# Loading w_up in two parts and regrouping the rows of w_down in a fused attention and feed-forward decode step

## The chip, the cores and the metric

One core of one Trainium2 chip runs the whole kernel in one launch. The metric is the device time of that core in microseconds, as a median over several executions. The six executions of the kernel before lie between 202.97 and 203.59 us, 0.3% or 0.6 us apart. The span that a profile shows is some 1.4 us shorter than the device time of the same execution (203.26 and 201.86 us before).

## The reference

A single token (640 features) goes through layernorm, attention over a cache of 32 heads with 4096 positions each, a residual, a second layernorm, and a gated feed-forward block with a residual. Weights and caches are bf16. Cut to what matters:

```
h  = x + attention(layernorm(x), k_cache, v_cache, wq, wo)
ln = layernorm(h)
g  = ln @ w_gate                 # 640 x 1728
u  = ln @ w_up                   # 640 x 1728
h2 = h + (gelu(g) * u) @ w_down  # 1728 x 640
```

With one token there is hardly any arithmetic per byte. The caches are 67 MB, all inputs together 84 MB, and each byte is used once.

## The kernel before

All large loads are issued by one engine (sync) on one queue (q1, 84.23 MB in the page), in the order wq, K and V caches by groups of four heads, wo, then the feed-forward weights. The feed-forward loads and the matmuls that use them are these; `P.dma(engine, out, in, *deps)` issues a transfer when its dependencies are done, and `T(fn, *deps)` runs matmuls when theirs are.

```python
d_w1 = P.dma("sync", wd_sb[:, 12, :], B_w_down[64:192, :], mults[NG - 1, 1])
for o in (0, 1, 2, 3, 32, 33, 34, 35):           # the first 64 rows of w_down, 8 loads of 10 KB
    ...
d_wg = P.dma("sync", wg_sb, B_w_gate[:, :].rearrange("(p c) n -> p c n", c=5), pvs[NG - 2])
d_wu = P.dma("sync", wu_sb, B_w_up[:, :].rearrange("(p c) n -> p c n", c=5))
d_wd = [P.dma("sync", wd_d[:, a, lo:hi, :], wd_v[:, a, lo:hi, :])
         for a, lo, hi in ((0, 0, 4), (1, 0, 4), (2, 0, 3), (2, 3, 4))]
... # cut: wo projection, second layernorm
def glu(ps, w, *ws):                             # 75 matmuls of one column each
    def fn(e):
        for c in range(5):
            for m in range(15):
                if m < 12:
                    ws = w[:, c, 192 + 512 * (m // 4) + m % 4:192 + 512 * (m // 4) + 512:4]
                elif m == 12:
                    ws = w[:, c, 64:192]
                else:
                    ws = w[:, c, 16 * m - 208:16 * m - 80]
                i = e.matmul(ps[:, m:m + 1], ws, hlnT[:, c:c + 1], ...)
        return i
    return T(fn, *ws)
ga = glu(ps_g, wg_sb, hl, d_wg)
up = glu(ps_u, wu_sb, d_wu)
... # cut: gelu on VectorE and ScalarE; hm = gelu(g) * u, needs ga and up
T(down([12]), g9, d_w1)                          # 4 matmuls per row block m, one per quarter of the output
T(down([13, 14]), d_wp)
T(down(range(4)), d_wd[0])
T(down(range(4, 8)), d_wd[1])
T(down(range(8, 11)), d_wd[2])
dn = {q: T(down([11], [q]), d_wd[3]) for q in (0, 2, 1, 3)}
... # cut: four copies of [1, 160] out of PSUM, two per engine; one store of the output row
```

A row of w_down is multiplied by one element of hm. Which partition a row of w_down lies in decides which column of w_gate and w_up must produce that element there, so regrouping the rows of w_down also changes the stride of the weights in `glu`.

The softmax here doesn't subtract the row's maximum and nothing guards it: scores larger than these inputs give would overflow.

Of the kernel before, what the change touches and what calls it, by code (L numbers as in the profile page):

```python
# [20 lines left out]
NG = 8  # L21
# [159 lines left out]
def bass_sequential_preLN__gqa_block_cached__glu_gated_geglu__decode_kernel(nc, A_x, A_k_cache, A_v_cache, A_wq, A_wo, B_x, B_w_gate, B_w_up, B_w_down, out):  # L181
# [49 lines left out]
    ps_g, ps_u, ps_p = bank[0], bank[1], bank[2]  # L231
# [10 lines left out]
    P = Prog(nc)  # L242
    V = lambda fn, *d: P.op("vector", fn, *d)
    A = lambda fn, *d: P.op("scalar", fn, *d)
    T = lambda fn, *d: P.op("tensor", fn, *d)
# [10 lines left out]
    mults, pvs = {}, {}  # L256
# [56 lines left out]
    def layernorm(src, ev, out_fn, between=lambda: None):  # L313
        s2 = V(lambda e: e.tensor_mul(src[:, 5:10], src[:, 0:5], src[:, 0:5]), ev)
        m = T(lambda e: e.matmul(ps_s[:, 16:26], mean_f[:, :], src[:, 0:10], start=True, stop=True), s2, c_mean)
        l1 = V(lambda e: e.reduce_sum(ln[:, 0:2], ps_s[:, 16:26].rearrange("p (a c) -> p a c", a=2), axis=AX.X), m)
        l2 = V(lambda e: e.scalar_tensor_tensor(out=ln[:, 2:3], in0=ln[:, 0:1], scalar=ln[:, 0:1],
                                                in1=ln[:, 1:2], op0=ALU.mult, op1=ALU.subtract), l1)
        l3 = A(lambda e: e.activation(ln[:, 3:4], ln[:, 2:3], ACTF.Ln, bias=eps_t[:, 0:1], scale=-1.0), l2, c_eps)
        l4 = A(lambda e: e.activation(ln[:, 4:5], ln[:, 3:4], ACTF.Exp, bias=zero_t[:, 0:1], scale=-0.5), l3)  # L320
        between()
        return V(out_fn, l4)
# [91 lines left out]
    for G in range(1, NG):  # L414
# [3 lines left out]
        for kind, g in order[3 + 2 * G:5 + 2 * G]:  # L418
# [8 lines left out]
                         start=True, stop=True), rt, c_ones)  # L427
# [7 lines left out]
                              start=True, stop=True), as_, c_of)  # L435
# [5 lines left out]
    wg_sb = v_slot[:, 0:5 * DF].rearrange("p (c n) -> p c n", c=5)  # L441
    wu_sb = v_slot[:, 5 * DF:10 * DF].rearrange("p (c n) -> p c n", c=5)
    wd_sb = k_slot[1][:, 0:15 * D].rearrange("p (m n) -> p m n", m=15)
    wd_v = B_w_down[192:1728, :].rearrange("(a p r) n -> p a r n", a=3, r=4)
    wd_d = wd_sb[:, 0:12, :].rearrange("p (a r) n -> p a r n", a=3)
    d_w1 = P.dma("sync", wd_sb[:, 12, :], B_w_down[64:192, :], mults[NG - 1, 1])
    for o in (0, 1, 2, 3, 32, 33, 34, 35):
        lo = o - o % 32
        d_wp = P.dma("sync", wd_lo[o:o + 13:4, :, :],
                     B_w_down[lo:lo + 32, :].rearrange("(r i q) n -> q i r n", q=4, r=2)[o - lo, :, :, :], c_wd, chan="wp")  # L450
    d_wg = P.dma("sync", wg_sb, B_w_gate[:, :].rearrange("(p c) n -> p c n", c=5), pvs[NG - 2])
    d_wu = P.dma("sync", wu_sb, B_w_up[:, :].rearrange("(p c) n -> p c n", c=5))
    d_wd = [P.dma("sync", wd_d[:, a, lo:hi, :], wd_v[:, a, lo:hi, :])
             for a, lo, hi in ((0, 0, 4), (1, 0, 4), (2, 0, 3), (2, 3, 4))]


    T(lambda e: e.matmul(ps_p[:, 0:5], id_f[:, :], xx[:, 0:5], start=True, stop=False, skip_group_check=True), xc, c_idf)
# [16 lines left out]
    def residual():  # L474
# [3 lines left out]
    hl = layernorm(hT, h, lambda e: e.tensor_scalar(  # L478
        hlnT[:, :], hT[:, 0:5], ln[:, 0:1], ln[:, 4:5], ALU.subtract, ALU.mult), residual)


    def glu(ps, w, *ws):
        def fn(e):
            for c in range(5):
                for m in range(15):
                    if m < 12:
                        ws = w[:, c, 192 + 512 * (m // 4) + m % 4:192 + 512 * (m // 4) + 512:4]
                    elif m == 12:
                        ws = w[:, c, 64:192]
                    else:  # L490
                        ws = w[:, c, 16 * m - 208:16 * m - 80]
                    i = e.matmul(ps[:, m:m + 1], ws, hlnT[:, c:c + 1],  # L492
                                 start=(c == 0 and m == 0), stop=(c == 4), skip_group_check=True)
            return i
        return T(fn, *ws)
    ga = glu(ps_g, wg_sb, hl, d_wg)

    up = glu(ps_u, wu_sb, d_wu)
    g1 = V(lambda e: e.tensor_tensor(out=g_t[:, :], in0=ps_g[:, 0:15], in1=own_g[:, :], op=ALU.mult), ga, c_gm)
    g2 = V(lambda e: e.tensor_mul(t1[:, :], g_t[:, :], g_t[:, :]), g1)  # L500
    g3 = V(lambda e: e.scalar_tensor_tensor(out=t2[:, :], in0=t1[:, :], scalar=1.0 / GELU_C1, in1=g_t[:, :],
# [5 lines left out]
    g9 = V(lambda e: e.tensor_mul(hm[:, :], gu[:, :], ps_u[:, 0:15]), g6, up)  # L507

    def down(ms, qs=range(4)):
        def fn(e):  # L510
            for m in ms:
                for q in qs:
                    rows, wd = (128, wd_sb[:, m]) if m < 13 else (48, wd_lo[:, m - 13])
                    i = e.matmul(ps_d[32 * q:32 * q + 1, 0:160], hm[0:rows, m:m + 1],  # L514
                                 wd[0:rows, 160 * q:160 * q + 160], start=False, stop=(m == 11))
            return i
        return fn
    T(down([12]), g9, d_w1)
    T(down([13, 14]), d_wp)
    T(down(range(4)), d_wd[0])  # L520
    T(down(range(4, 8)), d_wd[1])
    T(down(range(8, 11)), d_wd[2])
    dn = {q: T(down([11], [q]), d_wd[3]) for q in (0, 2, 1, 3)}
    os = [V(lambda e, q=q: e.tensor_copy(out_row[0:1, 160 * q:160 * q + 160], ps_d[32 * q:32 * q + 1, 0:160]), dn[q])  # L524
          for q in range(2)]
    os += [A(lambda e, q=q: e.copy(out_row[0:1, 160 * q:160 * q + 160], ps_d[32 * q:32 * q + 1, 0:160]), dn[q])
# [33 lines left out]
```

## Time and profile before

| | before |
|---|---|
| device time, median of 6 | 203.00 us (202.97 to 203.59) |
| span of the profiled execution (203.26 us) | 201.9 us |
| loaded from HBM | 84.23 MB, 417 GB/s over the span |
| busy: TensorE, VectorE | 60%, 50% |
| transfer engines | 97.6% |

In the views, PE is TensorE (matmuls), PEld its weight loads, DVE VectorE, ACT ScalarE, and SP the sync engine, which issues the large transfers. A transfer counts as landed here when the last of its completion counts in the trace has come; those of w_up came between 192.52 and 194.62 us in the trace before. Slack is the time between the landing of some data and the moment they are needed.

The page's chain of work that ended last, by line, names two loads and then compute. "L492" is `glu`, "L514" the down projection:

```profile
DMA v_slot<-in_A_v_cache_dram 55%; DMA v_slot<-in_B_w_up_dram 13%; PE psum L363 8%; DVE prod L375 7%; PE psum L167 6%; SPq L59 3%; DVE sc L381 2%; PE psum L492 1%; PE psum L514 1%; PE psum L352 1%; DVE out_row L524 0%; DVE hm L507 0%; DVEq L114 0%
```

The last load on it is w_up; the w_down loads issued behind w_up are not on it. The chain shows one path, the one that came last at each step, and hides how close the second was. The remaining lines, the utilisation and the timeline of the tail, stand in the prediction.

### The profile page before, as it was taken

How to read it: one execution, taken by the hardware profiler on the slowest of the kernel's cores; microseconds unless marked ns; L12 is line 12 of the kernel's file. 1: busy time of each engine (PE TensorE's matmuls, PEld its weight loads, DVE VectorE, ACT ScalarE, POOL GpSimd, SP SyncE). 2: the span in 40 equal slices, each digit the busy share in tenths (PEclk: the TensorE clock that was granted, in tenths of full speed). 3: DMA queues.
4: the chain of work that ended last, by engine and by line, in shares of the span. 5: the costliest groups of instructions: out<-in, count | busy, mean ns of one | idle time of the engine just before them, and what ended most of it. 6: DMA issues, size and time to landing. Idle time of an engine off the chain costs nothing.

```text
span 201.9 us, 2002 instructions
## 1 busy us (share of the span) xinstructions
PE 121.4 (60%) x1008; PEld 34.7 (17%) x756; DVE 100.9 (50%) x51; ACT 12.6 (6%) x33; POOL 30.6 (15%) x36
## 2 busy tenths in 40 slices
PE   0108009849408980994379166934990786779665
PEld 0101000001200120112011101020120012279563
DVE  0110197885598039906960993089519914120321
ACT  2010100001000100010000000100100010100101
POOL 6400000000010007101700450026006300100000
PEclk9999999999955698599579755995797599555555
DMA  9999999999999999999999999999999999999991
GB/s 341 422 425 435 429 422 429 416 474 425 429 422 422 422 448 448 435 416 429 422 422 474 422 429 422 429 416 474 429 429 416 429 422 444 402 419 444 428 387 61
DMA packets 3848, 84.30 MB, mean 418 GB/s; under 512 B 450, under 2 KB 772, under 8 KB 1156
## 3 DMA queue, kind: packets, MB, share of 16 engines
q1 hardware_dynamic: 3842, 84.23, 97.6%
q8 instruction: 4, 0.07, 0.1%
q10 hardware_dynamic: 2, 0.00, 0.0%
HBM read 84.23 MB, written 0.00 MB: 417 GB/s over the span
## 4 chain that ended last, share of the span: by engine, by line
DMA 68%; PE 18%; DVE 10%; SPq 3%; issue 1%; DVEq 0%
DMA v_slot<-in_A_v_cache_dram 55%; DMA v_slot<-in_B_w_up_dram 13%; PE psum L363 8%; DVE prod L375 7%; PE psum L167 6%; SPq L59 3%; DVE sc L381 2%; PE psum L492 1%; PE psum L514 1%; PE psum L352 1%; DVE out_row L524 0%; DVE hm L507 0%; DVEq L114 0%
## 5 line engine op out<-in xcount | busy, mean ns | idle before, releaser
L375 DVE TENSOR_TENSOR prod<-k_slot,qb 128x8192 bf16<-128x8192 bf16 x16 | 75.2, 4734 | 7.0 <-DMA k_slot<-in_A_k_cache_dram 5.2
L167 PE MATMUL psum<-prod,id_b 128*128 128x512 bf16 x233 | 65.4, 437 | 0.0
L381 DVE TENSOR_REDUCE sc<-psum 128x128 f32<-128x2048 f32 x8 | 18.3, 2291 | 49.1 <-PE psum L167 49.1
L352 PE MATMUL psum<-prod,id_b 128*128 128x512 bf16 x23 | 10.7, 467 | 50.5 <-DVE prod L375 47.1
L385 POOL TENSOR_TENSOR p_bd<-pt,own 128x512 bf16<-128x512 bf16 x6 | 24.4, 4071 | 89.5 <-ACT pt L382 89.5
L363 PE MATMUL psum<-v_slot,p_bd 128*16 128x512 bf16 x224 | 18.2, 484 | 5.1 <-DMA v_slot<-in_A_v_cache_dram 5.0
L352 PEld LDWEIGHTS psum<-prod,id_b 128*128 128x128 bf16 x23 | 2.3, 100 | 72.4 <-DVE prod L375 50.4
L369 PEld LDWEIGHTS psum<-hs,po_sb 128*128 128x128 f32 x64 | 9.1, 208 | 23.9 <-issue 23.4
L363 PEld LDWEIGHTS psum<-v_slot,p_bd 128*16 128x16 bf16 x224 | 5.8, 105 | 36.0 <-DMA v_slot<-in_A_v_cache_dram 27.9
L369 PE MATMUL psum<-hs,po_sb 128*128 128x4 f32 x64 | 8.5, 256 | 0.1
L392 ACT COPY po_sb<-psum 128x512 f32<-128x512 f32 x7 | 4.1, 586 | 71.8 <-PE psum L363 71.8
L382 ACT ACTIVATE pt<-sc,zero_t 128x128 bf16<-128x128 f32 x8 | 3.2, 401 | 71.2 <-DVE sc L381 71.2
L335 PE MATMUL psum<-arena,xlnB 128*32 128x512 bf16 x20 | 3.3, 627 | 6.2 <-DMA arena<-in_A_wq_dram 6.2
L462 PE MATMUL psum<-aP,arena 128*128 128x1 bf16 x160 | 6.7, 178 | 0.1
L462 PEld LDWEIGHTS psum<-aP,arena 128*128 128x128 bf16 x160 | 6.6, 131 | 0.2 <-DMA arena<-in_A_wo_dram 0.2
L492 PE MATMUL psum<-hlnT,v_slot 128*128 128x1 bf16 x150 | 5.1, 171 | 1.8 <-DMA v_slot<-in_B_w_up_dram 1.8
L389 POOL MEMSET spare<- 1x1 f32 x1 | 0.1, 90 | 36.6 <-DVE p_bd L385 36.6
L492 PEld LDWEIGHTS psum<-hlnT,v_slot 128*128 128x128 bf16 x150 | 5.0, 116 | 2.4 <-DMA v_slot<-in_B_w_up_dram 1.9
L308 PE MATMUL psum<-one_bf,x_row 1*128 1x1 bf16 x5 | 0.4, 177 | 8.3 <-DMA x_row<-in_A_x_dram 8.3
L363 PE MATMUL psum<-k_slot,p_bd 128*16 128x512 bf16 x32 | 3.6, 629 | 2.9 <-DVE p_bd L385 2.9
L340 DVE CAST qb<-psum 128x512 bf16<-128x512 f32 x1 | 0.7, 692 | 9.1 <-PE psum L167 9.1
L311 DVE COPY xx<-psum 128x5 f32<-128x5 f32 x1 | 0.2, 165 | 8.7 <-PE psum L308 8.7
(72 smaller groups left out, 35.1 us busy)
## 6 DMA issues: line engine op xcount, KB each, us to landing
k_slot<-in_A_k_cache_dram SPq DMA_DIRECT2D x8, 4096.0 KB, 25.5
v_slot<-in_A_v_cache_dram SPq DMA_DIRECT2D x7, 4096.0 KB, 16.7
arena<-in_A_wq_dram SPq DMA_DIRECT2D x1, 5120.0 KB, 15.8
arena<-in_A_wo_dram SPq DMA_DIRECT2D x2, 2560.0 KB, 34.5
k_slot<-in_A_v_cache_dram SPq DMA_DIRECT2D x1, 4096.0 KB, 26.1
v_slot<-in_B_w_gate_dram SPq DMA_DIRECT2D x1, 2160.0 KB, 21.3
v_slot<-in_B_w_up_dram SPq DMA_DIRECT2D x1, 2160.0 KB, 25.9
k_slot<-in_B_w_down_dram SPq DMA_DIRECT2D x2, 640.0 KB, 27.6
```

The costliest lines, as they stand in the source:

```text
L59: ev = self.op(eng, lambda e: e.dma_start(out, in_), *deps, dma=True, chan=chan)
L167: built = e.matmul(out, lhsT, rhs, start=start, stop=stop)
L335: mm = held if hf else lambda e, *a, **k: e.matmul(*a, **k)
L352: mm = held if n or not first else lambda e, *a, **k: e.matmul(*a, **k)
L363: i = e.matmul(ps_o[a:a + 16, :], p_bd[:, 4 * b:4 * b + 4, :].rearrange("p g j -> p (g j)"), vt[:, 4 * b:4 * b + 4, :], start=(b < 4), sto ...
L369: i = e.matmul(ps_a[:, bass.ds(at, 4)], po_sb[:, 128 * r:128 * r + 128], hs[:, r, :], start=(r == 0), stop=(r == 3))
L375: mults[G, i] = VM(lambda e: e.tensor_tensor(out=prod[:, i, :, :], in0=kt[:, 64 * i:64 * i + 64, :], in1=qb[:, G, :].unsqueeze(1).to_broad ...
L381: reds[G] = VR(lambda e: e.reduce_sum(sc[:, :], ps_f.rearrange("p (g d) -> p g d", d=16), axis=AX.X), folds[G, 1])
L385: blocks[G] = on(lambda e: e.tensor_tensor(out=p_bd[:, :, :], in0=pt[:, :].unsqueeze(2).to_broadcast([128, 128, 4]), in1=own[:, :].unsquee ...
L392: evs[G] = AS(lambda e: e.copy(po_sb[:, :], ps_o), pvs[G])
L462: r = e.matmul(ps_p[:, c:c + 1], wo_sb[:, i, c::5], aP[:, i:i + 1], start=False, stop=(i == 31), skip_group_check=True)
L492: i = e.matmul(ps[:, m:m + 1], ws, hlnT[:, c:c + 1], start=(c == 0 and m == 0), stop=(c == 4), skip_group_check=True)
```

## The change

Its intent is to shorten what can only start when w_up has landed: with w_up in two loads, three fifths of the up projection can run before the rest is in. And the rows of w_down, behind the first 64, are regrouped in blocks of 4, 4 and 5 rows per partition, so that the small load of rows 64 to 191 goes away. The diff, cut to its core:

```diff
-    d_w1 = P.dma("sync", wd_sb[:, 12, :], B_w_down[64:192, :], mults[NG - 1, 1])
+    blocks_d = ((64, 0, 4), (576, 4, 4), (1088, 8, 5))
+    at_row = {m0 + r: (lo + r, k) for lo, m0, k in blocks_d for r in range(k)}
+    def down_load(j, lo, hi): ...    # rows lo:hi of each partition of block j, after mults[NG - 1, 1]
...
-    d_wu = P.dma("sync", wu_sb, B_w_up[:, :].rearrange("(p c) n -> p c n", c=5))
-    d_wd = [P.dma("sync", wd_d[:, a, lo:hi, :], wd_v[:, a, lo:hi, :])
-             for a, lo, hi in ((0, 0, 4), (1, 0, 4), (2, 0, 3), (2, 3, 4))]
+    wu_v = B_w_up[:, :].rearrange("(p c) n -> p c n", c=5)
+    d_wu = [P.dma("sync", wu_sb[:, lo:hi, :], wu_v[:, lo:hi, :]) for lo, hi in ((0, 3), (3, 5))]
+    d_wd = [down_load(0, 0, 4), down_load(1, 0, 4), down_load(2, 0, 4), down_load(2, 4, 5)]
...
-                    if m < 12:
-                        ws = w[:, c, 192 + 512 * (m // 4) + m % 4:192 + 512 * (m // 4) + 512:4]
-                    elif m == 12:
-                        ws = w[:, c, 64:192]
+                    if m < 13:
+                        lo, k = at_row[m]
+                        ws = w[:, c, lo:lo + 127 * k + 1:k]
...
-    ga = glu(ps_g, wg_sb, hl, d_wg)
-    up = glu(ps_u, wu_sb, d_wu)
+    ga = glu(ps_g, wg_sb, range(5), hl, d_wg)
+    glu(ps_u, wu_sb, range(3), d_wu[0])
+    up = glu(ps_u, wu_sb, range(3, 5), d_wu[1])
...
-    T(down([12]), g9, d_w1)
-    T(down([13, 14]), d_wp)
+    T(down([13, 14]), g9, d_wp)
     T(down(range(4)), d_wd[0])
     T(down(range(4, 8)), d_wd[1])
-    T(down(range(8, 11)), d_wd[2])
-    dn = {q: T(down([11], [q]), d_wd[3]) for q in (0, 2, 1, 3)}
+    T(down(range(8, 12)), d_wd[2])
+    dn = {q: T(down([12], [q]), d_wd[3]) for q in (0, 2, 1, 3)}
```

More of the change, by code (lines that the diff above doesn't have):

```diff
@@ L443, in bass_sequential_preLN__gqa_block_cached__glu_gated_geglu__decode_kernel, with down_load @@
     wd_sb = k_slot[1][:, 0:15 * D].rearrange("p (m n) -> p m n", m=15)
-    wd_v = B_w_down[192:1728, :].rearrange("(a p r) n -> p a r n", a=3, r=4)
-    wd_d = wd_sb[:, 0:12, :].rearrange("p (a r) n -> p a r n", a=3)
-    d_w1 = P.dma("sync", wd_sb[:, 12, :], B_w_down[64:192, :], mults[NG - 1, 1])
+    blocks_d = ((64, 0, 4), (576, 4, 4), (1088, 8, 5))
+    at_row = {m0 + r: (lo + r, k) for lo, m0, k in blocks_d for r in range(k)}
+    def down_load(j, lo, hi):
+        row, m0, k = blocks_d[j]
+        return P.dma("sync", wd_sb[:, m0 + lo:m0 + hi, :],
+                     B_w_down[row:row + 128 * k, :].rearrange("(p r) n -> p r n", r=k)[:, lo:hi, :], mults[NG - 1, 1])
     for o in (0, 1, 2, 3, 32, 33, 34, 35):
@@ L479, in bass_sequential_preLN__gqa_block_cached__glu_gated_geglu__decode_kernel, with glu @@
         hlnT[:, :], hT[:, 0:5], ln[:, 0:1], ln[:, 4:5], ALU.subtract, ALU.mult), residual)
-    def glu(ps, w, *ws):
+    def glu(ps, w, cs, *deps):
         def fn(e):
-            for c in range(5):
+            for c in cs:
                 for m in range(15):
-                    if m < 12:
-                        ws = w[:, c, 192 + 512 * (m // 4) + m % 4:192 + 512 * (m // 4) + 512:4]
-                    elif m == 12:
-                        ws = w[:, c, 64:192]
+                    if m < 13:
+                        lo, k = at_row[m]
+                        ws = w[:, c, lo:lo + 127 * k + 1:k]
                     else:
@@ L494, in fn @@
             return i
-        return T(fn, *ws)
-    ga = glu(ps_g, wg_sb, hl, d_wg)
-    up = glu(ps_u, wu_sb, d_wu)
+        return T(fn, *deps)
+    ga = glu(ps_g, wg_sb, range(5), hl, d_wg)
+    glu(ps_u, wu_sb, range(3), d_wu[0])
+    up = glu(ps_u, wu_sb, range(3, 5), d_wu[1])
     g1 = V(lambda e: e.tensor_tensor(out=g_t[:, :], in0=ps_g[:, 0:15], in1=own_g[:, :], op=ALU.mult), ga, c_gm)
@@ L514, in fn @@
                     i = e.matmul(ps_d[32 * q:32 * q + 1, 0:160], hm[0:rows, m:m + 1],
-                                 wd[0:rows, 160 * q:160 * q + 160], start=False, stop=(m == 11))
+                                 wd[0:rows, 160 * q:160 * q + 160], start=False, stop=(m == 12))
             return i
         return fn
-    T(down([12]), g9, d_w1)
-    T(down([13, 14]), d_wp)
+    T(down([13, 14]), g9, d_wp)
     T(down(range(4)), d_wd[0])
     T(down(range(4, 8)), d_wd[1])
-    T(down(range(8, 11)), d_wd[2])
-    dn = {q: T(down([11], [q]), d_wd[3]) for q in (0, 2, 1, 3)}
+    T(down(range(8, 12)), d_wd[2])
+    dn = {q: T(down([12], [q]), d_wd[3]) for q in (0, 2, 1, 3)}
     os = [V(lambda e, q=q: e.tensor_copy(out_row[0:1, 160 * q:160 * q + 160], ps_d[32 * q:32 * q + 1, 0:160]), dn[q])
```

## The prediction

Passages that no trace or run of this case shows are cut from the prediction, and the cuts marked.

> **What bounds the kernel now.** I read the utilisation by slices first, then the chain of work that ended last, then the timeline of the last 12 us, then issue and landing of single transfers.
>
> ```profile
> DMA  9999999999999999999999999999999999999991
> GB/s 341 422 425 435 429 422 429 416 474 425 429 422 422 422 448 448 435 416 429 422 422 474 422 429 422 429 416 474 429 429 416 429 422 444 402 419 444 428 387 61
> ...
> q1 hardware_dynamic: 3842, 84.23, 97.6%
> ...
> DMA 68%; PE 18%; DVE 10%; SPq 3%; issue 1%; DVEq 0%
> ```
>
> The transfer engines are busy in 39 of 40 slices, and only the last slice (61 GB/s) is a tail. Two things alone can change the time: the sum of transfer work, or what happens after the last weights land. 84.23 MB over 97.6% of 201.9 us on 16 engines is 26.7 GB/s per engine.
>
> The tail, from the timeline:
>
> ```profile
> 190.27 2.57 PE L492 MATMUL psum<-hlnT,v_slot 128*128 128x1 bf16 x75
> ...
> 194.67 2.58 PE L492 MATMUL psum<-hlnT,v_slot 128*128 128x1 bf16 x75 [1.83 <-DMA v_slot<-in_B_w_up_dram]
> 197.35 0.17 DVE L507 TENSOR_TENSOR hm<-gu,psum 128x15 bf16<-128x15 f32 x1 [2.84 <-PE psum L492]
> 197.58 0.30 PE L514 MATMUL psum<-k_slot,hm 128*1 128x160 bf16 x4 [0.33 <-DVE hm L507]
> 197.81 0.43 PE L514 MATMUL psum<-wd_lo,hm 48*1 48x160 bf16 x8
> 198.18 1.77 PE L514 MATMUL psum<-k_slot,hm 128*1 128x160 bf16 x48
> 199.97 0.66 DVE L524 CAST out_row<-psum 1x160 bf16<-1x160 f32 x2 [2.45 <-PE psum L514]
> ```
>
> The reader is to see that the up projection waits 1.83 us for w_up, and that the down projection then runs without a wait on a transfer. The chain therefore ends w_up, up, hm, down, copy, store. It names no w_down transfer, but that does not say by how much w_down was early. For that I added the issue time of each transfer and its time to landing; here the first and the last of the four w_down loads behind w_up, with the issue line of the last:
>
> ```profile
> DMA to landing us min/median/max: 27.0/27.0/27.0
> ...
> 171.74 7.58 SPq L59 DMA_DIRECT2D k_slot<-in_B_w_down_dram  x1
> ...
> DMA to landing us min/median/max: 27.6/27.6/27.6
> ```
>
> The four were issued at 169.15, 169.62, 171.26 and 171.74, took 27.0, 28.1, 27.7 and 27.6, and landed at about 196.2, 197.7, 198.9 and 199.3. In the stream of 48 down matmuls one row block (4 matmuls, side by side) comes every 0.127 us (starts of single matmuls in the trace; 12 blocks in the 1.77 us, less 0.34 us for the last one to run through, give 0.13), so the blocks of these loads were due at 198.18, 198.66, 199.20 and 199.60. Their slack was 2.0, 0.9, 0.25 and 0.3 us. That is the number on which this prediction rests: whatever the up projection gains, the end can move by some 0.3 us before w_down takes over.
>
> [...] gate 189.5 (168.20 + 21.3), w_up 194.6 (168.68 + 25.9), then w_down in order of issue. [...] from 194.62 to the end the windows hold 158 + 403 + 371 + 210 + 46 KB = 1.19 MB, but the four w_down loads are 1.97 MB, so fast engines had moved 0.78 MB of w_down before w_up was declared landed. [...] single starts in the gate projection are 27 ns apart at stride 1 and 33 at stride 4, and the output projection, at stride 5, has 40.
>
> **The change part by part.**
> 1. *w_up in two loads.* Same bytes, 17,280 per partition as 10,368 and 6,912. It adds one packet per partition, 8 per engine. Packets in the trace cost about 26.95 GB/s plus 7 ns (5,120 bytes 196 ns, 3,840 bytes 149 ns, 1,280 bytes 55 ns), so +0.06 us per engine.
> 2. *w_down row block 12.* The 160 KB load that sat ahead of the small loads and w_gate goes away, and its rows join the last block. Ahead of w_gate, 160 KB (164 thousand bytes) over 16 engines at 26.7 GB/s, 0.38 us, disappear: w_gate, w_up and the first two w_down loads land 0.4 us earlier. The third w_down load grows from 3 rows to 4, so up to its end the queue holds the same bytes as before: still 198.9. The fourth still lands at 199.3. Two packets per partition (3,840 and 1,280 bytes, 204 ns) become one of 5,120 (196 ns): -0.06 us, which cancels part 1.
> 3. *Order of issue.* The removed load was where the sync queue waited for the last multiply (162.34). Now the eight small loads go out some 15 us earlier and w_gate at about 164 (when the seventh group's values are used) instead of 168.2. But w_gate is 5.3 us of transfer and landed 21.3 us after issue: some 16 us of other work stood ahead of it. Issuing earlier into a queue that never empties gives nothing.
> 4. *Strides of the weights.* Per input chunk, before: 12 matmuls at stride 4 and 3 at stride 1, 12 x 33.3 + 3 x 27 = 481 ns. After: 8 at stride 4, 5 at stride 5, 2 at stride 1, 8 x 33.3 + 5 x 40 + 2 x 27 = 520 ns. Five chunks: +0.2 us for gate and +0.2 us for up.
> 5. *The tail anew.* Gate is released by the layernorm and still starts at 190.27; its matmuls take 2.60. Up's first three chunks follow without a wait at 192.87, because three fifths of w_up (3.1 of the 5.16 us between the landings of w_gate and w_up) are in at 192.2. They end at 194.43. The last two chunks are in at 194.2 to 194.3, just in time, and end in another 1.04, at 195.47, against 197.08 before. Up is 1.6 us earlier. hm and the first down matmul follow 0.5 us later, as before (197.08 to 197.58), at 195.97. The small rows take 0.37 us to 196.34; the first w_down load (195.8) is in, 0.5 us to 196.9. **Here the new waits begin:** the second load lands at 197.3 (0.4 us lost), its four row blocks end at 197.9; the third lands at 198.94 (1.0 us lost). From 198.98 its four blocks run to 199.46, and the fourth load (199.31) is in. The last block starts at about 199.46 instead of 199.60.
>
> Sum: 1.6 us gained at up, about 1.45 us given back to waits for w_down, 0.14 us left, carried one to one through copies and store. 202.98 - 0.14 = **202.84 us**.
>
> **The rivals.** *The gain of up arrives whole.* For it: the chain names w_up and not w_down. If w_down had been in, the end would come 1.6 us earlier, 201.4 us (0.8%). Against it: 0.25 and 0.3 us of slack in the last two loads. *Slower, because work moved from an early transfer into the last one.* The last block now waits for five rows per partition. If the last landing came 0.38 us later, the end would be at about 203.1 to 203.3. Against it: all loads share one queue that is full, so a load taken out in front advances everything behind it by what it took. *Earlier issue frees the stream.* If there were gaps around 162 to 168 us, closing them would shift all landings and the end by as much. Against it: 402 to 444 GB/s in those slices; only the dip at 402 (171.6 to 176.7) leaves some 0.2 us. *Stride 5 costs more than said.* Up would need over 1.5 us more before it touched the end, since the path now runs through w_down.
>
> **Range and chances.** All likely outcomes lie between 201.4 and 203.3, less than 1% away, so a change of over 2% (4 us) needs something that no view shows. Three runs before spread over 0.6 us, more than my effect. [...] I take 202.84 with 202.2 to 203.5, and chances of 0.02 faster, 0.97 within, 0.01 slower.
>
> **What would show it right or wrong.** Right: up starts at about 192.9 and no longer waits for w_up; down starts 1.5 us earlier and its three later groups wait for w_down, about 0.4 and 1.0 us; the chain now ends in a w_down transfer; the first copy is at 199.8. The gate's 75 matmuls take 0.2 us longer. Wrong: the last w_down landing is not at 199.3 but clearly off, which would carry the end with it; or a wait stands in front of the second part of up; or down still runs without a wait, which would mean that w_down lands over a microsecond earlier than I say.

## The result, and the profile after

| | before | after |
|---|---|---|
| device time, median of 6 | 203.00 us | 202.99 us (202.83 to 203.55) |
| ratio | | 0.9996, 95% interval 0.998 to 1.0013: the same |
| span of the profiled execution | 201.9 us | 201.4 us |

Ratios in this document are the mean time of one kernel's runs over that of the other's of the same rounds, so not quite the ratio of the medians quoted. The 0.5 us between the two profiled spans lies within the scatter of executions: others of the kernel before had spans of 201.4 to 201.8 us, those of the changed kernel 201.4 to 201.6. Times of day in the two traces are therefore compared from an event that the change does not touch, the landing of the second half of w_o: 183.91 us before, 183.61 after, so the profiled execution after is 0.3 us ahead before the change begins.

From the page after, the utilisation, the queue and the chain by engine and by line:

```profile
DMA  9989999999999999999999999999999999999992
...
q1 hardware_dynamic: 3842, 84.23, 97.8%
...
DMA 85%; PE 10%; SPq 4%; issue 0%; DVE 0%
DMA v_slot<-in_A_v_cache_dram 71%; DMA k_slot<-in_B_w_down_dram 13%; PE psum L363 9%; SPq L59 4%; PE psum L516 0%; DVE out_row L525 0%
```

The bytes and the share of busy transfer engines are as before. But where the chain had w_up at 13% and two projections behind it, it now has w_down at 13%, and neither `glu` nor hm is on it. The tail of the timeline after (start, duration, engine, line, operation, in brackets the idle time ahead of it and what ended it):

```profile
189.97 5.15 PE L494 MATMUL psum<-hlnT,v_slot 128*128 128x1 bf16 x144
...
195.78 0.37 PE L494 MATMUL psum<-hlnT,v_slot 128*128 128x1 bf16 x6 [0.67 <-issue]
196.26 0.17 DVE L509 TENSOR_TENSOR hm<-gu,psum 128x15 bf16<-128x15 f32 x1 [1.86 <-PE psum L494]
...
196.49 0.43 PE L516 MATMUL psum<-wd_lo,hm 48*1 48x160 bf16 x8 [0.33 <-DVE hm L509]
...
196.85 1.23 PE L516 MATMUL psum<-k_slot,hm 128*1 128x160 bf16 x32
198.69 0.49 PEld L516 LDWEIGHTS psum<-k_slot,hm 128*1 128x1 bf16 x20 [0.95 <-DMA k_slot<-in_B_w_down_dram]
...
199.55 0.66 DVE L525 CAST out_row<-psum 1x160 bf16<-1x160 f32 x2 [3.12 <-PE psum L516]
```

The reader is to see three things. Gate and up are now one stream of 144 matmuls with no wait on w_up in it. Down starts at 196.49 instead of 197.58; less the 0.3 us by which this execution was ahead, that is 0.8 us earlier. And before its last 20 matmuls TensorE's weight loads stand for 0.95 us until the third w_down load is in; that wait did not exist before. What was gained at w_up was given back at w_down. There is also something the prediction did not have: the stream stops after 144 matmuls. By the starts of single matmuls it stands for 0.84 us, and the view puts that down to no wait at all ("issue").

The time from issue to landing of the first and the last of the four w_down loads after, with the issue of the first, and from the chain after the third load and the matmuls that it released (start, duration):

```profile
165.41 14.19 SPq L59 DMA_DIRECT2D k_slot<-in_B_w_down_dram  x4
...
DMA to landing us min/median/max: 30.1/30.1/30.1
...
DMA to landing us min/median/max: 26.9/26.9/26.9
...
171.63 27.02 DMA k_slot<-in_B_w_down_dram
...
198.69 0.88 PE psum L516 x18
```

The first landed at 165.41 + 30.1 = 195.5, the last, issued at 172.10, at 199.0. From the landing of w_o to the last landing it is 15.40 us before (199.31 - 183.91) and 15.42 after (199.03 - 183.61). The wait on the path is for the third load, though: it landed 15.03 us behind w_o before (198.94) and 15.04 after (198.64). The fourth, at 199.03, was in before its row block started at 199.17.

### The profile page after: what moved, and what is told of

The parts are those of the page before. It is cut to its first block, busy times and chain, and to the rows that moved or that the text cites. A ratio compares the mean times of both kernels' runs of the same rounds, so it can differ in the third digit from the quotient of the medians.

```text
span 201.4 us, 2003 instructions
## 1 busy us (share of the span) xinstructions
PE 119.7 (59%) x1009; PEld 33.8 (17%) x756; DVE 100.9 (50%) x51; ACT 12.6 (6%) x33; POOL 34.4 (17%) x36
## 4 chain that ended last, share of the span: by engine, by line
DMA 85%; PE 10%; SPq 4%; issue 0%; DVE 0%
DMA v_slot<-in_A_v_cache_dram 71%; DMA k_slot<-in_B_w_down_dram 13%; PE psum L363 9%; SPq L59 4%; PE psum L516 0%; DVE out_row L525 0%
## 5 line engine op out<-in xcount | busy, mean ns | idle before, releaser
L385 POOL TENSOR_TENSOR p_bd<-pt,own 128x512 bf16<-128x512 bf16 x6 | 28.3, 4716 | 87.2 <-ACT pt L382 87.2
L369 PEld LDWEIGHTS psum<-hs,po_sb 128*128 128x128 f32 x64 | 8.3, 191 | 24.1 <-issue 23.5
L369 PE MATMUL psum<-hs,po_sb 128*128 128x4 f32 x64 | 7.7, 244 | 0.4 <-ACT po_sb L428 0.4
## 6 DMA issues: line engine op xcount, KB each, us to landing
k_slot<-in_B_w_down_dram SPq DMA_DIRECT2D x3, 640.0 KB, 30.1
```

Source lines behind the costliest of these rows:

```text
L369: i = e.matmul(ps_a[:, bass.ds(at, 4)], po_sb[:, 128 * r:128 * r + 128], hs[:, r, :], start=(r == 0), stop=(r == 3))
L385: blocks[G] = on(lambda e: e.tensor_tensor(out=p_bd[:, :, :], in0=pt[:, :].unsqueeze(2).to_broadcast([128, 128, 4]), in1=own[:, :].unsquee ...
```

## The experiments

Theory: the end is the landing of the last w_down loads plus the work that can only follow it, and the change touches neither by more than a tenth or two. Rivals: the gain of up arrives whole and something else eats it; or the bytes moved into the last load come later; or the two parts of the change help and hurt and cancel. "Correct" below is what the record says of the check of the result. It says so of the two kernels that are wrong, too, so it does not vouch for which rows of w_down are multiplied. That the changed kernel pairs rows and columns rightly can be read from the index arithmetic in its diff; no run shows it.

**Only w_up in two loads.** The loads and blocks of w_down, and so the strides, stay as before.

```diff
-    d_wu = P.dma("sync", wu_sb, B_w_up[:, :].rearrange("(p c) n -> p c n", c=5))
+    d_wu = [P.dma("sync", wu_sb[:, lo:hi, :], wu_v[:, lo:hi, :]) for lo, hi in ((0, 3), (3, 5))]
...                                          # cut: glu in three calls, as in the changed kernel
```

> The kernel before with w_up in two loads, w_down as before. Theory (w_down takes over): up ends about 1 us earlier than before (the profile before has it at 197.3), the down matmuls then wait for the last two w_down loads, the last down block starts at about 199.4 instead of 199.6, time within 0.3 us of before (about 202.8). Rival (the gain of up arrives whole): about 201.5 to 202, and no wait of down on a transfer.

Measured: 202.80 us against 203.03, ratio 0.9986 (0.997 to 1.0003), correct. The part of up behind the second load, and the end of down, in its timeline:

```profile
194.72 0.94 PE L493 MATMUL psum<-hlnT,v_slot 128*128 128x1 bf16 x24 [0.46 <-DMA v_slot<-in_B_w_up_dram]
...
198.98 0.71 PE L515 MATMUL psum<-k_slot,hm 128*1 128x160 bf16 x16 [0.43 <-DMA k_slot<-in_B_w_down_dram]
```

Behind the landing of w_up 30 matmuls are left instead of 75 (24 of them in this line). Down then waits for w_down. Its first matmul starts 1.05 us earlier than before (196.53 against 197.58), its last row block only 0.2 us (199.39 against 199.60; w_o landed at the same time in both to 0.01 us), about the slack of 0.25 to 0.3 us that the prediction had read. The rival of a gain that arrives whole falls.

**Only the blocks of w_down.**

```diff
...                                          # cut: d_wu is one load, as before
-    glu(ps_u, wu_sb, range(3), d_wu[0])
-    up = glu(ps_u, wu_sb, range(3, 5), d_wu[1])
+    up = glu(ps_u, wu_sb, range(5), d_wu)
```

> The changed kernel with w_up in one load again: the w_down blocks alone. Theory: w_up lands 0.4 us earlier in the stream, gate and up each take 0.2 us longer at stride 5 (75 matmuls in 2.6 us or more instead of 2.4), the last w_down landing does not move; time within 0.3 us of before (about 202.9). Rival (bytes moved from an early load into the last one land later): 203.2 to 203.4, with the last w_down landing later by 0.4 us against the landing of w_wo.

Measured: 202.84 us against 203.03, ratio 0.9994 (0.9975 to 1.0014), correct. Its up projection and the wait in its down projection:

```profile
194.07 2.74 PE L493 MATMUL psum<-hlnT,v_slot 128*128 128x1 bf16 x75 [0.93 <-DMA v_slot<-in_B_w_up_dram]
...
198.74 0.49 PEld L514 LDWEIGHTS psum<-k_slot,hm 128*1 128x1 bf16 x20 [0.34 <-DMA k_slot<-in_B_w_down_dram]
```

The 75 matmuls take 2.74 us against 2.58 before: the wider stride costs 0.16 us. From the landing of w_o, w_gate lands 5.13 us later (before 5.55, so 0.42 earlier) and the last w_down load 15.35 us later (before 15.40). The bytes moved behind did not make the last load later. Both halves of the change are the same as before within their intervals, which reach to some 0.6 us less and 0.3 more. The traces are finer: counted from the landing of w_o, the last block of down starts 0.20 us earlier than before with the split alone, 0.19 with the blocks alone and 0.12 with both. No half hurts, so this is no help and hurt that cancel.

**Does the split pay when there is no w_down to wait for?** Two kernels, both from the kernel before and both wrong: the four w_down loads behind w_up are left out, and down multiplies the one early block 13 times. They differ in the split of w_up alone.

```diff
-    d_wd = [...]                                       # both kernels: the four loads left out
-    rows, wd = (128, wd_sb[:, m]) if m < 13 else ...
+    rows, wd = (128, wd_sb[:, 12]) if m < 13 else ...
...                                                    # cut: down no longer waits for d_wd
-    d_wu = P.dma(...)                                  # second kernel alone
+    d_wu = [P.dma(...) for lo, hi in ((0, 3), (3, 5))]
...                                                    # cut: glu in three calls
```

> The kernel before without the four w_down loads behind w_up (down multiplies the one early block 13 times: a wrong result on purpose, same matmuls), w_up in one load. Theory: the chain of before ran through w_up, not through w_down, so the time is that of before within 0.3 us, with 1.97 MB less to load. Rival (the stream's total alone sets the time): 4.6 us less, about 198.4.

> The same with w_up in two loads of 3 and 2 rows. Theory: with no w_down to wait for, the split pays whole: up ends 45 matmuls (about 1.5 us) earlier after the same landing, so 1.2 to 1.6 us less than with one load, about 201.5. If the 0.84 us hole in the matmul stream of the changed kernel, which no transfer of weights explains, comes here too, 0.7 us less. Rival (the split is worth little by itself, for instance because the first part lands late too): within 0.3 us of one load.

Measured: with one load 203.02 us, ratio to before 1.0007 (0.9985 to 1.0029); with two loads 201.70 us, ratio 0.9939 (0.9922 to 0.9955). The timeline with one load, then with two:

```profile
194.45 2.57 PE L490 MATMUL psum<-hlnT,v_slot 128*128 128x1 bf16 x75 [1.79 <-DMA v_slot<-in_B_w_up_dram]
...
197.96 1.77 PE L512 MATMUL psum<-k_slot,hm 128*1 128x160 bf16 x48
```

```profile
194.50 1.12 PE L491 MATMUL psum<-hlnT,v_slot 128*128 128x1 bf16 x30 [0.35 <-DMA v_slot<-in_B_w_up_dram]
...
196.55 1.77 PE L513 MATMUL psum<-k_slot,hm 128*1 128x160 bf16 x48
```

This pair settles the main question. Leaving out 1.97 MB, 2.3% of all bytes, changes nothing as long as w_up comes in one load: before, the path ran through w_up and the compute behind it. With w_down out of the way the split moves the main block of down by 1.41 us (197.96 to 196.55) and the time by 1.3 us. The split works as meant, and the pause in the matmul stream did not come in either kernel. In the real kernel those 1.3 us meet the landing of w_down, and the pause.

**w_down ahead of w_up.** Same loads, other order.

```diff
-    d_wu = [...]
     d_wd = [...]
+    d_wu = [...]
```

> The changed kernel with the four w_down loads issued ahead of the two w_up loads: same bytes, same loads, other order. Theory (the end is the last landing plus the work that can only follow it): the last landing stays at about 199.0, behind it come 30 up matmuls, hm and all 60 down matmuls, some 3.3 us more than now, so about 206. Rival (only the sum of the bytes counts, the tail is small anyway): within 0.3 us of the changed kernel.

Measured: 206.32 us, ratio 1.0159 (1.0143 to 1.0176), correct.

```profile
199.22 1.21 PE L494 MATMUL psum<-hlnT,v_slot 128*128 128x1 bf16 x30 [0.34 <-DMA v_slot<-in_B_w_up_dram]
...
201.12 1.91 PE L516 MATMUL psum<-k_slot,hm 128*1 128x160 bf16 x52
```

The stream ends where it did (last landing 15.47 us behind that of w_o), but now 30 up matmuls, hm and all of down come after it: 3.3 us more, as expected. With equal bytes the order in the queue mattered here by these 3.3 us, what was left to do behind the last of them.

**More work in up.** 20 more matmuls, result unused, behind the changed kernel's up projection.

```diff
     up = glu(ps_u, wu_sb, range(3, 5), d_wu[1])
+    up = T(more)       # more, cut: 20 matmuls of one column into an unused column of PSUM
```

> The changed kernel with 20 more matmuls of 33 ns (0.67 us, result unused) right behind the up projection. Theory (the end hangs on w_down, up has 0.9 us of slack): down starts 0.67 us later and waits that much less, time within 0.15 us of the changed kernel (about 203.0). Rival (the path still runs through up): 0.67 us more, about 203.6.

Measured: median 202.94 us over six runs, against 202.96 before. Five runs lie between 202.91 and 203.62; one at 205.55 widens the interval (ratio 1.0027, 0.9988 to 1.0065):

```profile
195.94 0.81 PE L502 MATMUL psum<-hlnT,v_slot 128*128 128x1 bf16 x20
...
198.77 0.49 PEld L521 LDWEIGHTS psum<-k_slot,hm 128*1 128x1 bf16 x20 [0.43 <-DMA k_slot<-in_B_w_down_dram]
```

The additional work came out of the wait for w_down: 0.95 us in the changed kernel, 0.43 here. Up is off the path.

**The pause in the matmul stream.** 20 more matmuls ahead of gate, to see whether the pause belongs to a place in the instructions or to the data.

```diff
         T(resid, hx)
+        T(ahead)       # ahead, cut: 20 matmuls of one column into an unused column of PSUM
```

> The changed kernel with 20 more matmuls (40 instructions, result unused) ahead of the gate projection. In the changed kernel the 150 matmuls of gate and up run without a pause up to the 144th, then stand for 0.84 us with nothing to wait for. Theory (the pause belongs to a place in the instruction stream, where a further 16 KB of instructions are fetched behind the weights): it comes 20 matmuls earlier, behind about the 124th, and a 16 KB instruction packet starts 2 to 3 us ahead of its end. Rival (it belongs to the data, for instance to the second part of w_up): it stays behind the 144th. The time stays within 0.3 us of the changed kernel in both.

Measured in one look (203.28 us, state unknown, correct):

```profile
190.84 4.40 PE L499 MATMUL psum<-hlnT,v_slot 128*128 128x1 bf16 x124
...
196.30 1.07 PE L499 MATMUL psum<-hlnT,v_slot 128*128 128x1 bf16 x26 [1.06 <-issue]
```

The pause came after the 124th matmul instead of the 144th, as it should if it belongs to a place in the instruction stream. But the 20 matmuls also delay the others, so the pause begins at nearly the same time (195.07 here, 194.94 there), and this run alone does not tell a place from a fixed time. Other traces do: the kernel before runs its up matmuls without a gap from 194.67 to 197.08, and in the one-copy kernel below the pause comes after the 144th matmul too, although that one starts 0.3 us later, counted from the landing of w_o (11.66 against 11.33 us). Here is the queue view of the changed kernel between 193.1 and 193.2 us, and of this kernel between 193.5 and 194.5:

```profile
q8 instruction: 1, 0.02, 64.0%
```

```profile
q8 instruction: 1, 0.02, 6.4%
```

In each, one packet of 16 KB of instructions starts on the transfer engines, at 193.14 and at 193.91, and the pause ends at 195.78 and 196.30: 2.6 and 2.4 us after. In the three other traces with the pause (only w_up split, more work in up, one copy) it is 2.4 to 2.5 us. The same pause came after the 144th matmul in the kernel with only w_up split (shorter there, because w_up was waited for first), and none is seen in the kernel before, where TensorE waits for w_up over that time. In the kernel without w_down and with two loads of w_up, whose TensorE instructions up to there are those of the kernel with only w_up split, that packet starts at 192.13 instead of 193.45, and there is no pause. The author's reading is a fetch of instructions held up by the w_down transfers. It stays inferred from the place and the timing, as does that the fetch ends the pause: no event in the trace ties them. The packet itself took 1.02 us in the changed kernel and was through at 194.16, 1.6 us before the pause ended; the other seven such packets in the traces before and after took 1.03 to 1.19 us. The pause cost nothing in the changed kernel, since down had to wait for w_down later. With 20 matmuls more in front of it, it took 1.23 us by the starts of matmuls (195.07 to 196.30) and used up what was left: down no longer waits for a transfer there, and the chain runs through the matmuls again.

**One copy in place of four**, an attempt at a version that beats both: what follows the last landing is on the path, so shorten it.

```diff
...                                           # cut: out4 replaces out_row
-    os = [...]                                # four copies of [1, 160], two per engine
-    d_out = P.dma("sync", out[0, :, :], out_row[:, :], *os)
+    cp = V(lambda e: e.tensor_copy(out4[:, :], ps_d[:, 0:160]), *dn.values())
+    d_out = P.dma("sync", out[0, :, :].rearrange("o (q n) -> (o q) n", q=4), out4[0:97:32, :], cp)
```

> The changed kernel with one copy of all 128 partitions out of PSUM in place of four of one partition (two per engine, 0.30 us each, one after the other), and the output stored from four partitions of 320 bytes. Theory (what is left behind the last landing is all on the path): 0.3 us less, about 202.7, if the store of four rows lands as fast as the store of one. Rival: the store of four rows takes longer than 0.3 us more and eats it, 203.0 or over.

Measured: 203.02 us, ratio 1.0001 (0.9989 to 1.0012), correct: a miss. The copy and the issue of the store:

```profile
199.71 0.32 DVE L525 CAST out<-psum 128x160 bf16<-128x160 f32 x1 [3.02 <-PE psum L516]
...
200.06 0.59 SPq L59 DMA_DIRECT2D out_dram<-out  x1
```

One copy takes 0.32 us where four took 0.66, but the issue of the store, now four rows of 320 bytes from four partitions, takes 0.59 us instead of 0.27 for one row of 1,280 bytes, and it lands 1.64 us after it began instead of 1.13 (by the completion counts in the traces). The rival was right: 0.5 us more in the store eats the gain. No version tried here beats both kernels by more than the scatter of the runs.

## Why the prediction was right

The forecast of 202.84 us, in a range of 202.2 to 203.5, with "within 2%" at 0.97, held: 202.99 us. The time alone is a weak test: every rival lay within 2% of before, and the one of later landings (203.1 to 203.3) in the range as well; only the gain that arrives whole (201.4) lay outside. What confirms the mechanism is the steps:

- *The slack of w_down is the number that counts.* Confirmed, and by the pair without w_down isolated: 1.3 us from the split where nothing stands behind it, none where w_down does.
- *Order and amount in the queue.* Confirmed. w_gate landed 0.43 us earlier (0.4 forecast); the third w_down load, on which the end hung, and the fourth did not move (15.03 and 15.04, 15.40 and 15.42 us from w_o). Put on the clock of the trace before (plus 0.3 us), the four landed at 195.8, 197.4, 198.9 and 199.3; forecast were 195.8, 197.3, 198.9 and 199.3. Issuing the small loads 15 us earlier (147.60 instead of 162.71) did not move these landings.
- *Strides.* Forecast +0.2 us per projection; measured 0.16 for up and 0.19 for gate with the blocks alone (2.74 and 2.76 us against 2.58 and 2.57). In the changed kernel most single starts are 27 to 28 ns apart at stride 1, 32 to 34 at stride 4 and 40 at stride 5.
- *Up and down.* This step failed in part: down was to start 1.6 us earlier, at 195.97, and started at 196.49 in an execution that was 0.3 us ahead, so 0.8 us earlier. The term that was missing is the pause of 0.84 us. It was harmless for the time because it was shorter than the slack it fell into. That was luck: a pause longer by more than the 0.8 us of wait that was left would have moved the end.
- *The waits of down.* Forecast 0.4 us for the second load and 1.0 for the third. The third came: weight loads stood for 0.95 us, and by the starts of matmuls 0.82 us were lost (0.94 between two starts, less the usual 0.12). The second did not, since the pause had already made down late.
- *The sum.* The landing of the third load plus the same work behind it, 0.14 us earlier than before. (Its 1.45 us of waits do not follow from its steps, which give 1.6 us when they are added without rounding. Nor does it count the 0.13 us by which down without waits became shorter, 2.02 us to its last block before and 1.89 by its own steps. The two errors cancel, and the end of 199.46 rests on the landing alone.) Set right by the 0.3 us that the profiled execution was ahead, the last block started 0.13 us earlier (199.17 + 0.3 against 199.60). In the times, -0.14 us can be neither shown nor refuted: the interval reaches from -0.4 to +0.3 us.

What stays open is why the transfer engines finish w_down so far apart: the completion counts of the last load spread over 2.0 us before (197.28 to 199.31) and 1.8 us after. The trace does not name the engines, so whether the load could be spread better was not tried.

## What to carry to other kernels

A chain of waits names the path that came last; before shortening it, list when the next input of the same tail lands and subtract, because here the gain was capped by that slack (0.25 to 0.3 us) and not by what was removed (1.3 us where nothing stood behind it). In this kernel, whose transfer engines were busy for 97.6% of the span, splitting or reordering loads was worth what it took away from behind the last landing: 1.3 us less with w_up in two loads and no w_down, 3.3 us more with w_up last. To test whether a part works at all, take away what it would run into, even at the price of a wrong result, and measure it there.
